# Attention probabilities: 32x32 turns on VectorE and 16 small DMAs in place of transposes on TensorE

## The chip, the cores and the metric

The kernel runs on one core of a Trainium2 chip. Its engines are TensorE (PE, whose weight loads are listed apart as PEld), VectorE (DVE), ScalarE (ACT), GpSimd (POOL) and SyncE (SP), which here only issues DMAs. The metric is the device time of one execution in microseconds. Three runs of the kernel before gave 952.71, 953.46 and 953.47 us, median 953.46.

## The reference

Eight batches of eight heads with 576 positions and head width 64 go through windowed attention: heads 0 to 3 look at the last 32 positions, heads 4 to 7 at every fourth of the last 128. The result goes token by token through an MLP with a rational activation.

```python
scores = scale * np.matmul(q, k.transpose(0, 1, 3, 2))
mask_plain = (rel >= 0) & (rel < window)
mask_dil = (rel >= 0) & (rel < window * dilation) & (rel % dilation == 0)
scores = np.where(masks[None, :, :, :], scores, -1000000000.0)
scores = scores - np.max(scores, axis=-1, keepdims=True)
attn = np.exp(scores)
attn = attn / (np.sum(attn, axis=-1, keepdims=True) + 1e-09)
return np.matmul(attn, v).astype(np.float32)
...
x = np.ascontiguousarray(attn_out.transpose(0, 2, 1, 3)).reshape(B * S, H * D)
...
h = x @ w_in
P = a[0] + a[1] * h + a[2] * h2 + a[3] * h3
Q = 1.0 + np.abs(b[0]) * np.abs(h) + np.abs(b[1]) * h2
g = P / (Q + 1e-06)
return (g @ w_out).astype(np.float32)
```

x has 4608 tokens of width 512; w_in is 512x2048 and w_out 2048x512.

## The kernel before

**Precision.** Every matmul operand of the MLP is split into a high and a low part (`xh`, `xl`, `gh`, `gl`, and two halves of each weight), and each product takes three matmuls: high times high, high times low, low times high.

**The MLP.** The tokens are cut into nine chunks `c` of 512 columns: chunk b (0 to 7) holds the first 512 tokens of batch b, chunk 8 the last 64 tokens of all batches (`x_left`). A chunk takes 16 tiles `ft` of 128 of the 2048 inner columns, 144 tiles in all (class `Tile`). A tile has 12 matmuls into an `h` bank (`Tile.h`), eleven steps of the activation on ACT, DVE and POOL, and 12 matmuls into four `out` banks, issued as four operations of three (`Tile.out`). Both halves are called "halves of a tile" below. Chunk 0 is done in two parts with its partial sums put aside in DRAM (`part`).

**Attention.** A batch is six units (class `Unit`), 48 units in all. Because of the window, and after the dilated heads' positions are put in order modulo 4, each group of 32 queries needs 64 keys. A unit's scores fill 128 partitions by six blocks of 64 keys. The unit's steps are: scores (PE); mask, maximum and subtraction (DVE); exponential (ACT); sum and reciprocal (DVE); `norm` (POOL); `transposes` (PE, three of 128x128 against an identity, into a PSUM bank); `place` (ACT or DVE, from the bank to the SBUF tile `pT`); `av`, attention times values (PE); and the evacuation of the result into `xh` (ACT) and `xl` (DVE).

**Two forms of a unit.** Batches below `ROWS` use matmuls of 128 rows by 64 columns (24 for the scores and 24 for `av`, counting both passes of a float32 matmul). The probabilities are placed in two copies of 64 partitions each into a tile that holds zeros in the other places. For some of these units (`ON_PE`) PE adds the mask by a matmul with the identity, and ACT takes the exponential bank by bank with the maximum as bias and the sum accumulated (`max_bank`, `exp_bank`), so that DVE has no mask, subtraction and sum to do. Batches from `ROWS` on (the attribute `rows`) use matmuls of 64 rows by 32 columns (48 for the scores, 96 for `av`) into two joined PSUM banks (`pair`); one copy places all of `pT`. These units start when all weights have been decoded, since the joined banks take the room of others. In the kernel before `ROWS` is 2.

**Order.** No engine chooses its order at run time. Class `Plan` simulates all operations ahead: each has the engines that may run it with a cost in ns, the operations that it needs, a rank (the time at which it is due, in tiles), and the buffers that it takes (`plan.takes`). The plan always starts what can start first, and of what can start within `WINDOW` ns the lowest rank. Each engine's instructions are then issued in the planned order and wait on semaphores for what they need. `DUE` gives for each batch when its last unit is due and the step between units; `LATE`, `SLACK`, `EARLY_TILES` and `PERIOD` shift ranks. A DMA is booked as its time on SP, then its bytes at 405 bytes per ns, then 1600 ns until it has landed. From the second unit of a form on, `av` of one unit and the scores of the next are one operation `sc` on PE; it needs `prev.placed`.

**SP.** One queue issues all DMAs: loads of q and k (`qk`), of v, of the weights, and stores of outputs from the tiles of the tag `stage` (four buffers, shared with the decoding of the weights). q/k and v have one buffer each, so a unit's loads are issued when the scores or `av` of the unit before have read theirs.

The lines that matter here: 300 to 308 (`scores_rows`), 392 to 403 (`av`), 363 to 389 (`exp` to `place`), 471 to 521 (the unit's operations), 541 to 548 (buffers), 823 and 824 (`pT`).

Of the kernel before, what the change touches and what calls it, by code (L numbers as in the profile page):

```python
# [18 lines left out]
P = 128  # L19
# [6 lines left out]
BOTH, ON_ACT, ON_DVE = {"ACT": 450, "DVE": 500}, {"ACT": 450}, {"DVE": 500}  # L26


ON_PE = [[1, 0, 0, 1, 1, 1], [1, 0, 1, 1, 1, 0], [0, 0, 0, 0, 0, 0], [0, 0, 0, 0, 0, 0], [0, 0, 0, 0, 0, 0], [0, 0, 0, 0, 0, 0], [0, 0, 0, 0, 0, 0], [0, 0, 0, 0, 0, 0]]
PLACE = [(ON_ACT, ON_DVE), (ON_ACT, ON_ACT), (ON_ACT, ON_DVE), (ON_DVE, ON_ACT), (ON_DVE, ON_ACT), (ON_DVE, ON_ACT), (ON_DVE, ON_ACT), (ON_DVE, ON_ACT)]  # L30
DUE = [(1.14, 0.78), (7.17, 0.52), (31.12, 3.35), (44.26, 2.11), (55.98, 1.84), (78.88, 1.84), (93.23, 1.71), (104.69, 0.27)]

LATE = {"ab": -19.97, "ql": -10.42, "pl": 5.4, "qq": 18.68, "t1": 4.2, "t2": -2.51, "ln": -22.56, "ex": -3.7, "g0": 1.26, "g1": 0.06, "g2": -6.38, "gh": -35.31, "gl": 12.35, "out": 3.53}
SLACK = {"sc": -0.4, "qk0": 0.66, "v0": 0.33, "load": -2.47, "wi": 2.03, "wo": 0.71, "w": 0.79, "gl": 0.63, "out": 2.59}

EARLY_TILES = 48

ROWS = 2
LEFT = S - 512
NQ, NKEY, NV = 2 * 6 * 64, 2 * 224, 3 * 2 * 2 * 64  # L40
RQ, RKEY = 4 * 3 * 32, 4 * 128
# [36 lines left out]
class Plan:  # L78
# [1 line left out]


    HOP = {"PE": 200.0, "ACT": 135.0, "DVE": 120.0, "POOL": 80.0, "SP": 0.0}
    TO_POOL, DUE_HOP, WINDOW = 70.0, 150.0, 100.0
    DMA_START, DMA_NS, DMA_RATE = 4000.0, 1600.0, 405.0
    PERIOD = 4051.0

    def __init__(self):
        self.ops, self.tags = [], {}
# [87 lines left out]
def tile_attention_moe(  # L176
# [32 lines left out]
    def mm(o, lhs, rhs, start=True, stop=True):  # L209
        pin(nc.tensor.matmul(o, lhs, rhs, start=start, stop=stop))  # L210
# [44 lines left out]
    class Unit:  # L255
# [97 lines left out]
        def sub(self, pool, tag):  # L353
            self.new_p(pool, tag)
            if self.rows:

                p = self.p.rearrange("p (i r) k -> p r i k", r=2)
# [19 lines left out]
        def transposes(self, tag):  # L377
            self.t = self.bank(tag, "t_ps")
            pf = self.p.rearrange("p j k -> p (j k)")
            for i in range(3):  # L380
                pin(nc.tensor.transpose(self.t[:, P * i : P * i + P], pf[:, P * i : P * i + P], ident))  # L381

        def place(self, half, eng):
            src = self.t[:, :384].rearrange("p (g q) -> p g q", q=32)
            if self.rows:
                copy(eng, pT_rows, self.t[:, :384].rearrange("p (i c) -> p i c", i=3))
                return
            dst = self.pT.rearrange("p i h e q -> p (i h e) q")
            lo = 64 * half
            copy(eng, dst[lo : lo + 64, :, 32 * half : 32 * half + 32], src[lo : lo + 64])  # L390

        def av(self, tag):
            v_t = self.v.rearrange("p (i h e d) -> p i h e d", i=3, h=2, e=2)
            if self.rows:
                for i in range(3):
                    for h in range(2):

                        for n in range(4):
                            for r in range(2):
# [69 lines left out]
        def plan(self, by, start):  # L469

            b, u = self.b, self.u
            alt = u % 2 if start else 0
            self.pT = pTs[alt]
            s_tag, t_tag, self.o_tag = start["banks"] if start else ("att", "att", "dec")
            (qp, qt), (kp, kt), (vpool, self.vt), (pp, pt) = start["tiles"] if start else ((att, "qk"), (att, "qk"), (att, "v"), (att, "p"))
            rows = self.rows
# [48 lines left out]
            if not start:  # L525
                sc.follows.append(Unit.last_read[0])
            Unit.last_read = [Unit.last_read[1], tr]
# [17 lines left out]
            plan.takes(tr, t_tag, PS_BUFS[t_tag], self.placed)  # L545
# [278 lines left out]
    pT_rows = pTs[0].rearrange("p i h e q -> p (i h e q)")[:, :384].rearrange("p (i c) -> p i c", i=3)  # L824
# [163 lines left out]
```

## Time and profile before

| | us |
|---|---|
| median of 3 runs | 953.46 |
| lowest, highest | 952.71, 953.47 |
| the profiled execution | 949.98 |
| its span, from the first to the last instruction | 948.2 |

In the page's rows an engine's name is followed by its busy time; a group's row gives the line, engine and operation, the tile written and the tiles read, the shape, the count, then busy time and mean ns of one, then the engine's idle time ahead of it and what ended it. Many instructions stand under the line of a helper (210 for matmuls, 213 for activations, 216 and 219 for additions and products on DVE, 222 for POOL, 207 for DMAs), so groups are told apart by their tiles: `p` are a unit's probabilities, `p_T` is the tile `pT`, `pair` the joined banks, `h` and `out` the banks of the MLP, `a`, `r`, `t` its intermediate tiles.

A matmul's row in a timeline runs until its modelled end; matmuls overlap, so what one costs is read from the start of the next. A DMA's row on SP is the issue alone; the data lands later.

### The profile page before, as it was taken

The numbers are of one execution on the slowest core, as the hardware profiler recorded it, in microseconds if no ns is written. First come the engines' busy times: TensorE is split into PE (matmuls) and PEld (weight loads), VectorE is DVE, ScalarE is ACT, GpSimd is POOL, SyncE is SP. The second block draws the span as 40 slices with busy tenths as digits, with TensorE's granted clock in tenths as the row PEclk, the third lists the DMA queues.
The fourth block names the chain that finished last, engine by engine and source line by source line (L and its number), as shares of the span: only waits on it lengthen the run. The fifth ranks groups of instructions, "written<-read, shape, count | busy, mean of one in ns | idle before, by whom it ended". The sixth has DMA issues, their size and how long they took to land.

```text
span 948.2 us, 22991 instructions
## 1 busy us (share of the span) xinstructions
PE 905.2 (95%) x9373; PEld 735.1 (78%) x9373; DVE 720.0 (76%) x1301; ACT 677.3 (71%) x1172; POOL 469.3 (49%) x409
## 2 busy tenths in 40 slices
PE   6699788999999999999999999999999999999998
PEld 5577566777778788878888887888888888888876
DVE  5989989667788777887577886778887577666655
ACT  4888788657666666767776767667677787777765
POOL 3666757554545454544544453444344445445442
PEclk9999999999999999999999999999999999999999
DMA  9745800013332212311022122122320010001001
GB/s 337 274 162 182 337 22 1 20 37 119 119 118 74 75 37 84 101 49 33 1 82 66 48 74 75 53 65 75 118 74 19 1 45 1 1 1 45 1 1 45
DMA packets 26025, 72.74 MB, mean 77 GB/s; under 512 B 3008, under 2 KB 3904, under 8 KB 25920
## 3 DMA queue, kind: packets, MB, share of 16 engines
q1 hardware_dynamic: 25920, 71.28, 21.7%
q8 instruction: 73, 1.20, 0.5%
q14 instruction: 32, 0.26, 0.1%
HBM read 60.79 MB, written 10.49 MB: 75 GB/s over the span
## 4 chain that ended last, share of the span: by engine, by line
PE 80%; DVE 10%; ACT 5%; issue 2%; DMA 1%; POOL 1%; SPq 0%; ACTq 0%; POOLq 0%; DVEq 0%
PE h L210 36%; PE out L210 36%; PE pair L210 6%; DVE a L219 2%; ACT r L213 1%; DVE h L219 1%; PE pair L381 1%; DVE xl L216 1%; PE s_ps L210 1%; ACT p L213 1%; DVE mx L337 1%; DVE t L216 1%; ACT t L213 1%; DVE wo_b L219 1%; ACT a L213 1%
## 5 line engine op out<-in xcount | busy, mean ns | idle before, releaser
L210 PE MATMUL h<-xh,wi 128*128 128x512 f32 x1136 | 379.7, 395 | 14.1 <-DVE a L219 12.4
L210 PE MATMUL out<-gh,wo 128*128 128x512 f32 x1136 | 357.8, 396 | 2.3 <-POOL wo L222 1.7
L222 POOL TENSOR_TENSOR a<-r,a 128x512 f32<-128x512 f32 x141 | 182.3, 1293 | 269.8 <-ACT r L213 261.3
L210 PEld LDWEIGHTS h<-xh,wi 128*128 128x128 f32 x1136 | 214.4, 189 | 64.0 <-DVE a L219 18.8
L210 PEld LDWEIGHTS out<-gh,wo 128*128 128x128 f32 x1136 | 208.9, 188 | 48.4 <-POOL wo L222 2.3
L210 PE MATMUL h<-xl,wi 128*128 128x512 f32 x568 | 222.7, 392 | 0.0
L210 PE MATMUL out<-gl,wo 128*128 128x512 f32 x568 | 221.8, 391 | 0.0
L222 POOL TENSOR_TENSOR gl<-a,gh 128x512 fp32r<-128x512 f32 x141 | 185.4, 1315 | 39.2 <-ACT gh L213 38.1
L219 DVE SCALAR_TENSOR_TENSOR a<-a,r 128x512 f32<-128x512 f32 x141 | 98.2, 697 | 114.6 <-ACT r L213 112.4
L213 ACT ACTIVATE r<-a,ln_bias 128x512 f32<-128x512 f32 x141 | 102.2, 725 | 72.5 <-POOL a L222 72.3
L213 ACT ACTIVATE a<-h 128x512 f32<-128x512 f32 x140 | 83.6, 597 | 87.1 <-PE h L210 86.4
L219 DVE SCALAR_TENSOR_TENSOR h<-h,na_t,r 128x512 f32<-128x512 f32 x142 | 107.0, 754 | 43.1 <-ACT r L213 43.0
L210 PEld LDWEIGHTS h<-xl,wi 128*128 128x128 f32 x568 | 107.4, 189 | 23.3 <-issue 2.1
L210 PEld LDWEIGHTS out<-gl,wo 128*128 128x128 f32 x568 | 106.7, 188 | 22.8
L213 ACT ACTIVATE r<-a,ab_t 128x512 f32<-128x512 f32 x141 | 114.7, 813 | 5.5 <-DVE a L219 3.5
L219 DVE SCALAR_TENSOR_TENSOR h<-t,na_t,h 128x512 f32<-128x512 f32 x142 | 107.2, 755 | 4.1
L213 ACT ACTIVATE t<-h,na_t 128x512 f32<-128x512 f32 x142 | 110.0, 774 | 0.1
L213 ACT ACTIVATE r<-r,exp_bias 128x512 f32<-128x512 f32 x144 | 103.8, 721 | 3.6
L216 DVE TENSOR_TENSOR t<-t,h 128x512 f32<-128x512 f32 x142 | 96.9, 682 | 11.2 <-ACT t L213 10.1
L213 ACT ACTIVATE gh<-a 128x512 fp32r<-128x512 f32 x123 | 77.7, 632 | 38.6 <-PE out L210 28.5
L219 DVE SCALAR_TENSOR_TENSOR a<-a,h 128x512 f32<-128x512 f32 x140 | 95.4, 682 | 2.5
L222 POOL TENSOR_TENSOR p<-p,sm 128x384 f32<-128x384 f32 x48 | 40.4, 841 | 79.3 <-DVE sm L372 42.9
(103 smaller groups left out, 726.0 us busy)
## 6 DMA issues: line engine op xcount, KB each, us to landing
v<-in_vp_dram SPq DMA_DIRECT2D x48, 384.0 KB, 3.7
qk<-in_qk_rows_dram SPq DMA_DIRECT2D x36, 448.0 KB, 4.6
out_dram<-os SPq DMA_DIRECT2D x36, 256.0 KB, 2.2
wi_raw<-in_w_in_dram SPq DMA_DIRECT2D x16, 512.0 KB, 8.1
wo_raw<-in_w_out_dram SPq DMA_DIRECT2D x16, 512.0 KB, 8.7
qk<-in_qk_dram SPq DMA_DIRECT2D x6, 608.0 KB, 5.0
q<-in_qk_dram SPq DMA_DIRECT2D x6, 384.0 KB, 6.8
k<-in_qk_dram SPq DMA_DIRECT2D x6, 224.0 KB, 7.0
```

The source lines that it names most:

```text
L210: pin(nc.tensor.matmul(o, lhs, rhs, start=start, stop=stop))
L213: pin(nc.scalar.activation(o, i, func, **kw))
L216: pin(nc.vector.tensor_tensor(o, x, y, op))
L219: pin(nc.vector.scalar_tensor_tensor(o, x, s, y, op0, op1))
L222: pin(nc.gpsimd.tensor_tensor(o, x, y, op))
L337: pin(nc.vector.tensor_reduce(mx, self.blocks(), axis=AX, op=ALU.max))
L381: pin(nc.tensor.transpose(self.t[:, P * i : P * i + P], pf[:, P * i : P * i + P], ident))
```

## The change

From batch 3 on, the units no longer use PE's transposes and the copy out of the bank. `turn` runs two DVE transposes, each on 128x192 elements: within each group of 32 partitions every 32x32 block of the probabilities is turned, and the result goes to a tile `turned` of the tag `stage`. `move` then issues 16 DMAs on SP from SBUF to SBUF, each of 32 partitions by 96 elements (12 KB), which bring block (g, n) from partitions 32g and columns 96n to partitions 32n and columns 96g of `pT`. Units with an odd number put `pT` into one of the two buffers of tag `p`, the others into the old tile. `av` reads its operand at other columns; its matmuls have the same number and shape. The subtraction writes `p` in the order (r, i) instead of (i, r).

Batch 2 goes back to the form of batches 0 and 1, with the mask on PE for five of its six units. In batch 1 the mask is on PE for six units instead of four; in batch 0 for four as before, but others. The constants of the plan (`PLACE`, `DUE`, `LATE`, `SLACK`, `EARLY_TILES`, `WINDOW`, `PERIOD`, and the cost of `sc`) are changed too. In the plan, the moves are booked at 2400 ns on SP and three times their bytes.

```diff
-ON_PE = [[1, 0, 0, 1, 1, 1], [1, 0, 1, 1, 1, 0], [0, 0, 0, 0, 0, 0], [0, 0, 0, 0, 0, 0], [0, 0, 0, 0, 0, 0], [0, 0, 0, 0, 0, 0], [0, 0, 0, 0, 0, 0], [0, 0, 0, 0, 0, 0]]
+ON_PE = [[0, 0, 1, 1, 1, 1], [1, 1, 1, 1, 1, 1], [1, 0, 1, 1, 1, 1], [0, 0, 0, 0, 0, 0], [0, 0, 0, 0, 0, 0], [0, 0, 0, 0, 0, 0], [0, 0, 0, 0, 0, 0], [0, 0, 0, 0, 0, 0]]
...
-DUE = [(1.14, 0.78), (7.17, 0.52), (31.12, 3.35), (44.26, 2.11), (55.98, 1.84), (78.88, 1.84), (93.23, 1.71), (104.69, 0.27)]
+DUE = [(0.94, 0.39), (7.47, 0.67), (31.59, 4.01), (46.12, 2.31), (58.3, 2.05), (80.22, 2.04), (96.72, 1.88), (106.06, 0.47)]
...
-EARLY_TILES = 48
-
-ROWS = 2
+EARLY_TILES = 36
+
+ROWS = 3
...
+        def turn(self):
+
+            self.turned = work.tile([P, 512], F32, tag="stage", name=f"u{self.n}", bufs=4)[:, :384]
+            src = self.p.rearrange("p (r i) (k a) -> p r k i a", r=2, k=2)
+            dst = self.turned.rearrange("p (r k i q) -> p r k i q", r=2, k=2, i=3)
+            for r in range(2):
+                pin(nc.vector.transpose(dst[:, r], src[:, r]))
+
+        def move(self):
+
+            if self.n % 2:
+                self.pT = att.tile([P, 6, 64], F32, tag="p", name=f"pT{self.n}", bufs=2).rearrange("p j k -> p (j k)")
+            else:
+                self.pT = pTs[0].rearrange("p i h e q -> p (i h e q)")[:, :384]
+            for n in range(4):
+                for g in range(4):
+                    load(self.pT[32 * n : 32 * n + 32, 96 * g : 96 * g + 96], self.turned[32 * g : 32 * g + 32, 96 * n : 96 * n + 96])
...
-                                c0, c1 = 192 + 96 * h + 32 * i, 64 * h + 32 * e
-                                mm(pair[0][32 * n : 32 * n + 32, r, c0 : c0 + 32], v_t[half, i, h, e, d], pT_rows[half, i, c1 : c1 + 32])
+                                c0, c1 = 192 + 96 * h + 32 * i, 96 * (2 * h + e) + 32 * i
+                                mm(pair[0][32 * n : 32 * n + 32, r, c0 : c0 + 32], v_t[half, i, h, e, d], self.pT[half, c1 : c1 + 32])
...
-                sc = op({"PE": 1370 if rows else 1750 + cost}, 0, lambda e: (prev.av(prev.o_tag), scores()), *prev.placed, prev.lv, *ready)
+                sc = op({"PE": 1650 if rows else 1750 + cost}, 0, lambda e: (prev.av(prev.o_tag), scores()), *prev.placed, prev.lv, *ready)
...
-            tr = op({"PE": 350 * cold}, 0, lambda e: self.transposes(t_tag), no, identity)
-            p0 = op(place0, 0, lambda e: self.place(0, e), tr, zeroed[alt], Unit.av_of.get(alt))
-            self.placed = [p0]
-            if not rows:
+            if rows:
+                tr = op({"DVE": 540}, 0, lambda e: self.turn(), no)
+                mv = op({"SP": 2400}, 0, lambda e: self.move(), tr, dma=P * 384 * 4 * 3)
+                self.placed = [mv]
+            else:
+                tr = op({"PE": 350 * cold}, 0, lambda e: self.transposes(t_tag), no, identity)
+                p0 = op(place0, 0, lambda e: self.place(0, e), tr, zeroed[alt], Unit.av_of.get(alt))
                 p1 = op(place1, 0, lambda e: self.place(1, e), tr, zeroed[alt], Unit.av_of.get(alt))
-                self.placed.append(p1)
+                self.placed = [p0, p1]
...
+            if rows:
+                plan.takes(tr, "stage", 4, [mv])
+            else:
+                plan.takes(tr, t_tag, PS_BUFS[t_tag], self.placed)
...
+            if self.rows:
+                plan.takes(self.placed[0], *(("p", 2) if self.n % 2 else ("pT", 1)), [av])
```

More of the change, by code (lines that the diff above doesn't have):

```diff
@@ L26 @@
 BOTH, ON_ACT, ON_DVE = {"ACT": 450, "DVE": 500}, {"ACT": 450}, {"DVE": 500}
-ON_PE = [[1, 0, 0, 1, 1, 1], [1, 0, 1, 1, 1, 0], [0, 0, 0, 0, 0, 0], [0, 0, 0, 0, 0, 0], [0, 0, 0, 0, 0, 0], [0, 0, 0, 0, 0, 0], [0, 0, 0, 0, 0, 0], [0, 0, 0, 0, 0, 0]]
-PLACE = [(ON_ACT, ON_DVE), (ON_ACT, ON_ACT), (ON_ACT, ON_DVE), (ON_DVE, ON_ACT), (ON_DVE, ON_ACT), (ON_DVE, ON_ACT), (ON_DVE, ON_ACT), (ON_DVE, ON_ACT)]
-DUE = [(1.14, 0.78), (7.17, 0.52), (31.12, 3.35), (44.26, 2.11), (55.98, 1.84), (78.88, 1.84), (93.23, 1.71), (104.69, 0.27)]
-LATE = {"ab": -19.97, "ql": -10.42, "pl": 5.4, "qq": 18.68, "t1": 4.2, "t2": -2.51, "ln": -22.56, "ex": -3.7, "g0": 1.26, "g1": 0.06, "g2": -6.38, "gh": -35.31, "gl": 12.35, "out": 3.53}
-SLACK = {"sc": -0.4, "qk0": 0.66, "v0": 0.33, "load": -2.47, "wi": 2.03, "wo": 0.71, "w": 0.79, "gl": 0.63, "out": 2.59}
-EARLY_TILES = 48
-ROWS = 2
+ON_PE = [[0, 0, 1, 1, 1, 1], [1, 1, 1, 1, 1, 1], [1, 0, 1, 1, 1, 1], [0, 0, 0, 0, 0, 0], [0, 0, 0, 0, 0, 0], [0, 0, 0, 0, 0, 0], [0, 0, 0, 0, 0, 0], [0, 0, 0, 0, 0, 0]]
+PLACE = [(BOTH, BOTH), (ON_ACT, ON_ACT), (ON_DVE, ON_ACT), (ON_ACT, ON_DVE), (ON_ACT, ON_DVE), (ON_ACT, ON_DVE), (ON_ACT, ON_DVE), (ON_ACT, ON_DVE)]
+DUE = [(0.94, 0.39), (7.47, 0.67), (31.59, 4.01), (46.12, 2.31), (58.3, 2.05), (80.22, 2.04), (96.72, 1.88), (106.06, 0.47)]
+LATE = {"ab": -8.55, "ql": -4.01, "pl": -1.52, "qq": -2.86, "t1": 1.53, "t2": -0.78, "ln": -21.92, "ex": -13.06, "g0": 2.39, "g1": 0.11, "g2": -10.17, "gh": -21.84, "gl": 13.45, "out": 3.38}
+SLACK = {"sc": -0.39, "qk0": -0.2, "v0": -0.54, "load": -2.56, "wi": 1.44, "wo": 0.87, "w": 0.4, "gl": 0.78, "out": 2.83}
+EARLY_TILES = 36
+ROWS = 3
 LEFT = S - 512
@@ L82 @@
     HOP = {"PE": 200.0, "ACT": 135.0, "DVE": 120.0, "POOL": 80.0, "SP": 0.0}
-    TO_POOL, DUE_HOP, WINDOW = 70.0, 150.0, 100.0
+    TO_POOL, DUE_HOP, WINDOW = 70.0, 150.0, 200.0
     DMA_START, DMA_NS, DMA_RATE = 4000.0, 1600.0, 405.0
-    PERIOD = 4051.0
+    PERIOD = 4743.0
     def __init__(self):
@@ L355, in sub @@
             if self.rows:
-                p = self.p.rearrange("p (i r) k -> p r i k", r=2)
+                p = self.p.rearrange("p (r i) k -> p r i k", r=2)
                 mx = self.mx.rearrange("p (r i) -> p r i", r=2)
@@ L381, in transposes @@
                 pin(nc.tensor.transpose(self.t[:, P * i : P * i + P], pf[:, P * i : P * i + P], ident))
+        def turn(self):
[12 more added lines that the diff above has]
+                    load(self.pT[32 * n : 32 * n + 32, 96 * g : 96 * g + 96], self.turned[32 * g : 32 * g + 32, 96 * n : 96 * n + 96])
         def place(self, half, eng):
             src = self.t[:, :384].rearrange("p (g q) -> p g q", q=32)
-            if self.rows:
-                copy(eng, pT_rows, self.t[:, :384].rearrange("p (i c) -> p i c", i=3))
-                return
             dst = self.pT.rearrange("p i h e q -> p (i h e) q")
@@ L472, in plan @@
             alt = u % 2 if start else 0
-            self.pT = pTs[alt]
+            if not self.rows:
+                self.pT = pTs[alt]
             s_tag, t_tag, self.o_tag = start["banks"] if start else ("att", "att", "dec")
@@ L526, in plan @@
                 sc.follows.append(Unit.last_read[0])
-            Unit.last_read = [Unit.last_read[1], tr]
+            Unit.last_read = [Unit.last_read[1], su if rows else tr]
             loads = (lq, lk, lv) if start else (lq, lv)
@@ L544, in plan @@
             plan.takes(sc, s_tag, PS_BUFS[s_tag], [su, *(clear[1:] if rows else [])])
-            plan.takes(tr, t_tag, PS_BUFS[t_tag], self.placed)
+            if rows:
+                plan.takes(tr, "stage", 4, [mv])
+            else:
+                plan.takes(tr, t_tag, PS_BUFS[t_tag], self.placed)
             plan.takes(su, pt, 2 if pp is att else 1, [tr])
```

1 line of the change is left out of this document (removed).

## The prediction

> **What bounds the kernel now.** I read the page first (busy shares, the 40 slices), then the busy time by stretches, then the chain that ended last.
>
> ```profile
> span 948.2 us, 22991 instructions
> PE 905.2 (95%) x9373; PEld 735.1 (78%) x9373; DVE 720.0 (76%) x1301; ACT 677.3 (71%) x1172; POOL 469.3 (49%) x409
> PE 80%; DVE 10%; ACT 5%; issue 2%; DMA 1%; POOL 1%; SPq 0%; ACTq 0%; POOLq 0%; DVEq 0%
> ```
> ```profile
> 100.00:175.00 75.00, 65.54 (x315) 50.51 (x315) 69.39 (x114) 58.99 (x97) 49.38 (x40) 0.98 0.24 92
> 175.00:300.00 125.00, 121.95 (x1737) 97.94 (x1740) 93.76 (x176) 82.20 (x136) 61.06 (x56) 1.00 0.25 81
> 300.00:700.00 400.00, 396.41 (x5109) 323.69 (x5098) 310.37 (x585) 278.44 (x457) 187.81 (x161) 1.00 0.20 66
> 700.00:930.00 230.00, 229.51 (x1381) 189.20 (x1380) 154.33 (x243) 172.55 (x265) 109.00 (x85) 1.00 0.05 16
> ```
> The columns of the second fence are the stretch, its length, then the busy time of PE, PEld, DVE, ACT and POOL, the clock and the DMA share. From 175 us to 930 PE is busy 747.9 of 755 us: TensorE is the bound there, and every microsecond of its work that goes is worth about one. From 100 to 175 DVE is (69.4 of 75), while PE idles 9.5. DVE has 22% free from 300 on, and the DMA engines 80%.
>
> What one attention unit costs PE is read from the chain in one dense stretch (start, length, what; x12 is half a tile of the MLP):
>
> ```profile
> 495.88 2.74 PE h L210 x12
> 498.62 2.73 PE out L210 x12
> 501.36 0.33 PE pair L381 x3
> 501.68 2.75 PE h L210 x12
> 504.44 1.45 PE pair L210 x91
> 505.89 2.94 PE out L210 x12
> 508.83 2.72 PE h L210 x12
> ```
> From 495.88 to 508.83 stand four halves (2.72 each undisturbed) and one unit: 12.95 - 10.88 = 2.07 us. The three transposes are 0.33 plus 0.03 by which the next half is longer: 0.36. The remaining 1.7 is attention times values with the next unit's scores (1.45, and 0.22 on the half behind it).
>
> **The change, part by part.**
>
> *Transposes off PE.* Batches 3 to 7 are 30 units: 30 x 0.36 = **-10.8 us**, all of it on the bound.
>
> *Turn on DVE.* The copy out of the bank goes, two transposes of 128x192 come.
>
> ```profile
> L225 DVE COPY p_T<-pair 128x384 f32<-128x384 f32 x30 | 16.6, 554 | 4.6 <-PE pair L381 4.6
> L216 DVE TENSOR_TENSOR pair<-pair,mask_t 128x192 f32<-128x192 f32 x36 | 13.2, 366 | 1.1
> ```
> Each is bounded by half the copy (0.28) and by the 128x192 addition (0.37); I take 0.28, since one input is read as in the copy, so 0.55 against 0.55. DVE's load stays, covered by the 22% that it has free; without that cover the dearer end would cost 30 x 0.18 = 5 us.
>
> *The 16 moves, and PE's new wait.* The matmuls of attention times values now wait for DMAs, not for DVE. Behind them in PE's queue stand the next scores and the MLP's matmuls, for which ACT and DVE wait in turn. The plan fixes the order ahead and books the moves at 2400 + 1456 + 1600 = 5456 ns (SP, bytes, landing). If they take longer, PE stands still by the excess, less the slack that the place in the order happens to leave. No row shows a DMA of 32 rows from SBUF to SBUF; the nearest are:
>
> ```profile
> L207 SPq DMA_DIRECT2D v<-in_vp_dram x48: 327/328/431, 4.5 to 718.3; - x48
> 34.73 0.33 SPq L207 DMA_DIRECT2D qk<-in_qk_dram  x1
> 35.10 1.10 SPq L207 DMA_DIRECT2D wo_raw<-in_w_out_dram  x1
> mask_t<-in_mask_dram SPq DMA_DIRECT2D x1, 96.0 KB, 2.0
> coef_t<-in_coef_dram SPq DMA_DIRECT2D x1, 3.0 KB, 1.7
> ```
> Issuing a DMA of 128 rows keeps SP 0.33 us, the next can start 0.37 after it, and up to 0.43 is seen behind another; the smallest lands 1.7 us after its issue. So from one move to the next it is 0.08 us (a quarter of 0.33 for a quarter of the rows) at the least and 0.48 (0.43 with the same pause) at the most; the 16th lands after 15 of these and 1.7: 2.9 to 8.9 us. I take 0.27, halfway, nearer to the alone-standing 0.33: part of that time should go with the rows. That is 5.75, with 0.2 for SP's pick-up 0.5 late against the booking. The slack is read from when the copy ended and when the matmuls began:
>
> ```profile
> 501.72 0.56 DVE L225 COPY p_T<-pair 128x384 f32<-128x384 f32 x1 [0.22 <-PE pair L381]
> 504.37 0.99 PE L210 MATMUL pair<-p_T,v 64*32 64x32 f32 x94
> 410.86 0.55 DVE L225 COPY p_T<-pair 128x384 f32<-128x384 f32 x1
> 411.71 0.99 PE L210 MATMUL pair<-p_T,v 64*32 64x32 f32 x94
> ```
> 2.09 and 0.30 us: it depends on whether a half of 2.72 us happened to run. I take it as evenly spread from 0 to 2.4. A lateness L then stalls PE by L x L / 4.8 on average: 0.05 us a unit for 0.5, **+2 us** in all, 0 to +72 at the ends (3.6 late is 2.4 a unit over the spread's mean of 1.2).
>
> The Trainium skill's page "DMA: Bandwidth & Descriptors", in the table under "Why a DMA increments its semaphore by 16 and not by 1", gives a copy's issue as 512 sequencer cycles whatever its size, in generations before the newest; with the 1.2 GHz of "Trainium Kernel Development and Optimization", Hardware Hierarchy, that is an estimate of 0.43 us an issue. The trace has 0.43 only behind another DMA and 0.33 alone; a fixed cost is the rule that speaks against this change, and the second rival below is its case.
>
> *Semaphores.* Where one writer was waited for, now up to 16 are.
>
> ```profile
> L381 PEldq EVENT_SEMAPHORE  x3: 51/51/51, 26.1 to 91.1; - x3
> ```
> A wait of its own costs PE's queue 51 ns: 0 to 16 x 0.051 = 0.82 us a unit. The first sixteen matmuls need all sixteen moves, many waits can be met while the array still has work, so I take two of them, 0.1 a unit: **+3 us**, 0 to +24.5 at the ends.
>
> *Moves in SP's queue.* They wait for the turn, and what stands behind them waits too: loads of the next unit and stores of outputs. Loads are issued behind the scores:
>
> ```profile
> 505.43 0.33 SPq L207 DMA_DIRECT2D v<-in_vp_dram  x1
> 505.92 1.47 SPq L207 DMA_DIRECT2D qk<-in_qk_rows_dram  x1
> 518.35 0.33 SPq L207 DMA_DIRECT2D v<-in_vp_dram  x1
> ```
> SP has nothing from 507.39 to 518.35, which is where the moves fall, so I cost this at 0. The cover is gone where an output store is placed ahead of the moves and its copy is late; then it is part of the lateness.
>
> A unit also becomes longer: from the transposes' start to its matmuls it took 504.37 - 501.36 = 3.0 us, and turn, pick-up and moves are 0.55 + 5.95 = 6.5. 30 x 3.5 = 105 us must fit between and behind the units:
>
> ```profile
> 425.62 1.22 SPq L207 DMA_DIRECT2D qk<-in_qk_rows_dram  x1
> 493.82 0.34 SPq L207 DMA_DIRECT2D v<-in_vp_dram  x1
> L225 DVE COPY x_left<-pair x30: 195/214/283, 226.7 to 733.8; 128x32 f32<-128x32 f32 x24, 128x128 f32<-128x128 f32 x6
> ```
> Between these two loads 68 us pass where the dense rhythm has 13: 55 us lie idle in the row of units. The last unit is out at 734, and the last 32 tiles need 32 x 5.44 = 174 us before the end at 948: 40 us more. 95 of the 105 are there in these two places alone, and smaller gaps stand between other batches, so I cost this at 0; without them 10 us of MLP would come late.
>
> *Batch 2 as in batch 1.* A unit there costs PE:
>
> ```profile
> 56.46 0.92 PE L210 MATMUL o_ps<-p_T,v 128*64 128x64 f32 x24
> 57.31 0.34 PE L210 MATMUL s_ps<-mask_t,ident_b 128*128 128x384 bf16 x1
> 57.58 0.92 PE L210 MATMUL s_ps<-qk 128*64 128x64 f32 x24
> 58.43 0.50 PE L210 MATMUL h<-xh,wi 128*128 128x512 f32 x1
> ```
> 0.85 + 0.27 + 0.85, with 0.36 of transposes 2.33, against 2.07 now. Five of six units add the mask on PE: 5 x 0.26 = **+1.3 us**; 0 to +3 with the pauses around it.
>
> *The start.* Batch 1 puts two more units' masks on PE, which takes from DVE the mask, the subtraction and the sum:
>
> ```profile
> L216 DVE TENSOR_TENSOR pair<-pair,mask_t 128x384 f32<-128x384 f32 x18 | 10.2, 564 | 0.6 <-ACT xh L213 0.2
> L216 DVE TENSOR_TENSOR p<-pair,mx 128x384 f32<-128x384 f32 x36 | 20.0, 555 | 0.8
> L368 DVE TENSOR_REDUCE sm<-p 128x6 f32<-128x384 f32 x40 | 22.0, 550 | 1.4 <-ACT p L213 1.2
> ```
> 2 x 1.67 = 3.3 us less on DVE where DVE is the bound; ACT takes them up. All ranks of the plan change as well, which can help or hurt the 9.5 us of PE's idle time there. I take **-1**, -4 to +4.
>
> The sum: -10.8 + 2 + 3 + 1.3 - 1 = -5.5 us. The profiled execution took 949.98 (948.2 of span and 1.8 around it), so 944.5 by its own measure; the median of the runs shown is 953.46, 3.5 above, and I put the same difference on it: **948.0 us**, 0.6% faster.
>
> **Rivals.**
>
> *The whole gain:* moves land within the booking, waits are met early, the start gives its 4 us. -10.8 + 1.3 - 4 = -13.5 at best, about 942 with half of it. For it: a quarter of the rows. Against: sixteen issues in 2.4 us is 0.15 each, under half of any issue in the trace.
>
> *Issue cost that does not shrink (slower):* each move keeps SP for 0.37 us as the 128-row DMAs do. The 16th lands after 15 x 0.37 + 1.7 + 0.2 = 7.5 us, 2.0 late; PE stands before attention times values 2.0 x 2.0 / 4.8 = 0.83 us a unit, +25 us: -10.8 + 25 + 3 + 1.3 - 1 = +17.5, about 971. It decides from the point where stalls eat 5.5 + 2 us, 0.25 a unit, 1.1 late, 0.31 us from one move to the next. For it: loads of different size (v, and qk at 34.73) take SP the same 0.33 us in the trace. Against: all of those have 128 rows.
>
> *Semaphores on PE:* all sixteen waits exposed, +24.5 for +3: 969. Against: the order lets PE's queue run ahead.
>
> *The start turns against it:* +4 for -1 and 1 to 2 more in batch 2: 953 to 956.
>
> **Chances.** Forecast 0.40 (its own range 943 to 953), whole gain 0.14, fixed issue cost 0.28, semaphores 0.06, start 0.12. About 0.2% (1.9 us) is what a measurement of this kernel can tell from no change. Faster: 0.33 of the forecast and 0.14; same: 0.07 of the forecast and 0.07 of the start; slower: 0.28 + 0.06 + 0.05. The range takes in the whole gain and the middle of the fixed issue cost: 941 to 974.
>
> **What would show it.** The transposes of line 381 fall from 48 units to 18, PE's busy time in 300 to 700 is filled by more tiles. Right is the forecast if the gap from the turn's end to the first matmul of attention times values is about 6 us and PE's waits for a DMA there sum to a few us. The slower rival shows as 16 issues on SP at 0.37 us and PE waiting for the last of them, 0.5 to 1 us in most of the 30 units. A lead of eight or more event waits on PE ahead of each unit would show the third. PE idle before 175 us beyond the 9.5 us of 100 to 175 shows the start wrong.

## The result, and the profile after

| | before | after |
|---|---|---|
| median (us) | 953.09 | 1132.61 |
| lowest, highest | 951.17, 953.47 | 1130.36, 1133.15 |
| the profiled execution: span | 948.2 | 1130.9 |
| mean granted clock of TensorE | 0.993 | 0.915 |

Four runs each. The ratio is 1.188 (95% interval 1.186 to 1.191): 18.8% slower. The forecast was 948.0 us and the range ended at 974.

The page of the kernel after, its busy shares, granted clock and chain:

```profile
span 1130.9 us, 22729 instructions
PE 981.9 (87%) x8717; PEld 789.0 (70%) x8717; DVE 733.7 (65%) x1320; ACT 691.5 (61%) x1244; POOL 473.1 (42%) x408
PEclk9899999998899988889998878988988899999999
PE 43%; SPq 17%; DVE 12%; ACT 9%; DMA 8%; issue 6%; POOL 4%; ACTq 0%; POOLq 0%; DVEq 0%
p_T<-u SPq DMA_DIRECT2D x240, 12.0 KB, 1.7
pT<-u SPq DMA_DIRECT2D x240, 12.0 KB, 1.8
```

SP's queue and DMAs, 1% of the chain before, are 25% of it now. The moves land 1.7 to 1.8 us after their issue, which is what the forecast took. PE has 656 instructions fewer, since the transposes and most of batch 2's small matmuls went, and yet it is busy for 77 us more: in the clock row stand many an 8 and a 7, and matmuls at a lower clock take longer.

The busy time by stretches of the kernel after (columns as before: stretch, length, PE, PEld, DVE, ACT, POOL, clock, DMA share, GB/s):

```profile
0.00:100.00 100.00, 78.01 (x770) 62.17 (x770) 81.13 (x167) 72.91 (x214) 57.82 (x66) 0.93 0.59 209
100.00:175.00 75.00, 68.88 (x325) 54.36 (x326) 67.90 (x102) 61.23 (x112) 46.41 (x38) 0.95 0.37 147
300.00:700.00 400.00, 335.50 (x3616) 268.39 (x3615) 234.24 (x446) 210.76 (x342) 137.50 (x114) 0.88 0.18 53
700.00:930.00 230.00, 188.76 (x2132) 151.23 (x2132) 130.94 (x251) 114.94 (x189) 74.40 (x61) 0.87 0.18 54
```

From 100 to 175 nothing is lost (PE 68.9 busy where it was 65.5). From 300 to 700 PE idles 64.5 us where it idled 3.6, at a clock of 0.88 where it was 1.00. The loss lies behind the start, where the units of batches 3 to 7 run.

One unit in the timeline (start, length, engine and line, what, and in brackets the idle time ahead and what ended it):

```profile
617.76 0.63 DVE L388 STREAM_TRANSPOSE u<-p 128x192 f32<-128x192 f32 x2
618.16 10.01 SPq L207 DMA_DIRECT2D p_T<-u  x16
624.88 0.24 PE L210 MATMUL pair<-p_T,v 64*32 64x32 f32 x2
627.51 0.34 PE L210 MATMUL pair<-p_T,v 64*32 64x32 f32 x8 [2.39 <-DMA p_T<-u]
628.23 0.41 PE L210 MATMUL pair<-p_T,v 64*32 64x32 f32 x8 [0.38 <-DMA p_T<-u]
628.83 0.41 PE L210 MATMUL pair<-p_T,v 64*32 64x32 f32 x8 [0.19 <-DMA p_T<-u]
630.03 0.92 PE L210 MATMUL pair<-p_T,v 64*32 64x32 f32 x69 [0.79 <-DMA p_T<-u]
631.63 1.22 PE L210 MATMUL out<-gh,wo 128*128 128x512 f32 x2
633.07 0.63 PE L210 MATMUL h<-xh,wi 128*128 128x512 f32 x1
633.50 0.63 PE L210 MATMUL h<-xl,wi 128*128 128x512 f32 x1
635.59 0.39 PE L210 MATMUL h<-xl,wi 128*128 128x512 f32 x1
635.82 0.63 PE L210 MATMUL h<-xh,wi 128*128 128x512 f32 x2
```

The reader is to see three things. First, SP is at the sixteen moves for 10.0 us, 0.63 each; the plan had booked 2.4 us there and 5.5 until all are landed. Second, PE arrives at 624.88 by the planned order, starts two matmuls whose move has landed, and stands still for 3.75 of the next five microseconds, released move by move; until 631.63 the unit keeps PE 6.75 us, where before it took 1.45 (504.44 to 505.89 in the prediction's chain). Third, after that stop the MLP's matmuls start 0.43 us apart (633.07, 633.50), and from about 635 on 0.23 again (635.59, 635.82): the clock had been lowered. The same unit by stretches (columns as above) shows the clock at 0.50 from 628.18 to 635.00:

```profile
624.80:628.18 3.38, 0.66 (x11) 0.36 (x10) 2.14 (x4) 1.77 (x3) 1.07 (x1) 1.00 0.08 18
628.18:635.00 6.82, 5.79 (x142) 4.77 (x143) 2.06 (x4) 1.34 (x3) 1.28 (x1) 0.50 0.39 124
635.00:640.00 5.00, 5.00 (x23) 4.12 (x23) 2.87 (x8) 2.97 (x6) 1.30 (x1) 1.00 0.04 14
```

The waits grouped (who, at what line, for what: us in total, times, longest):

```profile
PE pair L210 <- DMA pT<-u: 54.8, 56, 3.5
PE pair L210 <- DMA p_T<-u: 48.5, 56, 3.6
PE pair L210 <- issue: 10.7, 7, 1.8
```

PE's waits for moves are 103.3 us in all; the forecast said "a few". Another 10.7 stand at the same units with no releaser named. Half of the moves on SP (min/median/max of one issue in ns, first and last start; the other half has the same median), beside the loads of v with 128 rows from DRAM:

```profile
L207 SPq DMA_DIRECT2D p_T<-u x240: 507/588/1434, 253.0 to 897.1; - x120
L207 SPq DMA_DIRECT2D v<-in_vp_dram x48: 327/333/1502, 13.0 to 900.0; - x48
```

A move of a quarter of the rows takes longer to issue than a full load: 0.588 us against 0.333.

### The profile page after: what moved, and what is told of

Its sections match the earlier page's. It is cut to its first block, busy times and chain, and to the rows that moved or that the text cites. A ratio compares the mean times of both kernels' runs of the same rounds, so it can differ in the third digit from the quotient of the medians.

```text
span 1130.9 us, 22729 instructions
## 1 busy us (share of the span) xinstructions
PE 981.9 (87%) x8717; PEld 789.0 (70%) x8717; DVE 733.7 (65%) x1320; ACT 691.5 (61%) x1244; POOL 473.1 (42%) x408
## 4 chain that ended last, share of the span: by engine, by line
PE 43%; SPq 17%; DVE 12%; ACT 9%; DMA 8%; issue 6%; POOL 4%; ACTq 0%; POOLq 0%; DVEq 0%
PE out L210 19%; PE h L210 18%; SPq L207 17%; ACT r L213 5%; PE pair L210 5%; DVE a L219 3%; DVE h L219 3%; DMA p_T<-u 3%; POOL a L222 2%; DMA pT<-u 2%; DMA v<-in_vp_dram 1%; ACT a L213 1%; DVE t L216 1%; POOL p L222 1%; DMA wi_raw<-in_w_in_dram 1%
## 5 line engine op out<-in xcount | busy, mean ns | idle before, releaser
L210 PE MATMUL h<-xh,wi 128*128 128x512 f32 x1136 | 391.1, 406 | 9.2 <-DVE a L219 8.8
L210 PE MATMUL out<-gh,wo 128*128 128x512 f32 x1136 | 374.1, 412 | 0.0
L210 PEld LDWEIGHTS h<-xh,wi 128*128 128x128 f32 x1136 | 223.9, 197 | 63.2 <-DVE a L219 12.2
L210 PEld LDWEIGHTS out<-gh,wo 128*128 128x128 f32 x1136 | 221.9, 199 | 50.8 <-issue 5.2
L210 PE MATMUL out<-gl,wo 128*128 128x512 f32 x568 | 230.2, 405 | 1.3 <-POOL gl L222 1.3
L210 PE MATMUL h<-xl,wi 128*128 128x512 f32 x568 | 229.1, 403 | 0.8 <-DVE xl L216 0.8
L219 DVE SCALAR_TENSOR_TENSOR a<-a,r 128x512 f32<-128x512 f32 x141 | 103.3, 732 | 115.2 <-ACT r L213 106.9
L210 PEld LDWEIGHTS out<-gl,wo 128*128 128x128 f32 x568 | 112.4, 198 | 26.7 <-POOL gl L222 1.9
L210 PEld LDWEIGHTS h<-xl,wi 128*128 128x128 f32 x568 | 112.1, 197 | 24.3 <-DVE xl L216 1.1
L216 DVE TENSOR_TENSOR pair<-pair,mask_t 128x192 f32<-128x192 f32 (+1 forms) x45 | 19.5, 433 | 117.0 <-ACT xh L213 116.0
```

What stands on the lines that cost most here:

```text
L216: pin(nc.vector.tensor_tensor(o, x, y, op))
L219: pin(nc.vector.scalar_tensor_tensor(o, x, s, y, op0, op1))
```

## The experiments

The theory: a move's issue costs 0.63 us because both its ends are in SBUF, sixteen need 10 us, and PE stops by what that exceeds the booking and the slack of the order. The rivals: the many small packets; a limit on transfers under way; the plan's new constants; the turn.

**The issue by itself.** A small kernel with nothing but DMAs on SP, in groups: sixteen SBUF to SBUF (eight of 32 rows, eight of 128), four of 128 x 96, eight of 64 rows; then sixteen from DRAM (32 and 128 rows), eight to DRAM, four from DRAM with four pieces a row, four SBUF to SBUF of 32 x 2 KB.

> No attention and no MLP: SP alone issues groups of DMAs of nine forms, 4 to 8 of each, one behind the other: SBUF to SBUF with 32, 64 and 128 partitions, DRAM to SBUF with 32 and 128, SBUF to DRAM with 32, and 32 partitions with four runs each or with 2 KB rows. In the changed kernel a 32-partition SBUF-to-SBUF issue took 0.588 us, in the kernel before a 128-partition load or store 0.33. Theory 1 (both ends in SBUF make it dear): SBUF to SBUF takes about 0.59 us with 32, 64 and 128 partitions alike, and 32 partitions to or from DRAM about 0.33. Theory 2 (few rows, or a start partition other than 0, make it dear): 32 partitions take about 0.59 us wherever the ends are, and 128 partitions from SBUF to SBUF 0.33. Theory 3 (the queue is full in the big kernel): here all forms take 0.33 to 0.43 us.

Its timeline on SP (start, time from the first to the end of the last, what, count):

```profile
1.42 10.16 SPq L27 DMA_DIRECT2D sb<-src  x16
11.62 2.53 SPq L27 DMA_DIRECT2D sb128w<-src  x4
14.20 5.07 SPq L27 DMA_DIRECT2D sb<-src  x8
19.31 7.75 SPq L27 DMA_DIRECT2D ld<-in_w_dram  x16
27.11 3.68 SPq L27 DMA_DIRECT2D far<-src  x8
30.82 1.84 SPq L27 DMA_DIRECT2D ld32x<-in_w_dram  x4
32.71 2.45 SPq L27 DMA_DIRECT2D sb32w<-src  x4
```

And the durations of one issue by form, as above:

```profile
L27 SPq DMA_DIRECT2D sb<-src x24: 569/594/600, 1.4 to 18.7; - x24
L27 SPq DMA_DIRECT2D ld<-in_w_dram x16: 419/426/718, 19.3 to 26.6; - x16
```

From SBUF to SBUF one takes 0.62 to 0.64 with its pause, on average of each group, whether it has 32, 64 or 128 rows and 192 bytes or 2 KB a row. With one end in DRAM it takes 0.46 to 0.48 (all but the first load), again whatever its rows and pieces. So rows, bytes and packets are ruled out; the pair of ends sets the price. The first theory's 0.33 for the forms with one end in DRAM was too low: behind another one an issue takes 0.42 to 0.43.

**PE's transposes put back into the kernel after.** All else, the constants, batch 2 and the masks on PE, is as after:

```diff
...
-                tr = op({"DVE": 540}, 0, lambda e: self.turn(), no)
-                mv = op({"SP": 2400}, 0, lambda e: self.move(), tr, dma=P * 384 * 4 * 3)
-                self.placed = [mv]
+                tr = op({"PE": 350}, 0, lambda e: self.transposes(t_tag), no, identity)
+                self.placed = [op(ON_DVE, 0, lambda e: self.place(0, e), tr, zeroed[alt], Unit.av_of.get(alt))]
...
```

> The changed kernel with the transposes on PE and the single copy (on DVE) put back from batch 3 on; batch 2's form, the masks on PE and all constants of the plan stay as changed. Theory (the moves are the cause, the rest of the change is worth little): within 1% of the kernel before, 945 to 962 us, so 170 to 188 us faster than the changed kernel. Rival (the new constants and batch 2's form cost a good part): 985 us or more.

954.74 us, ratio 1.002 (1.001 to 1.003) to before. The constants, batch 2 and the start together, with an order of their own, are worth about 2 us of loss (0.7 to 3.2); turn and moves hold the rest of the 180.

**All the moves, but nobody waits for them.** The sixteen moves are issued as after, into places that are not read; attention times values reads a tile that holds zeros.

```diff
-                self.pT = pTs[0].rearrange("p i h e q -> p (i h e q)")[:, :384]
+                self.pT = pTs[0].rearrange("p i h e q -> p (i h e q)")[:, 384:]
...
-                                mm(..., self.pT[half, c1 : c1 + 32])
+                                mm(..., pTs[0].rearrange("p i h e q -> p (i h e q)")[half, c1 : c1 + 32])
```

> The changed kernel in the same planned order with all turns and all 480 moves, but the moves go to places that nobody reads, and attention times values reads a tile of zeros that is long there: the attention's result is left out, only PE's wait for the moves is gone. Theory (PE standing still for the moves, and the slower clock behind each stop, are all of the loss): 935 to 955 us, granted clock back at 0.98 or more. Rival 1 (the moves disturb others: SP's queue late for loads and stores, DMA traffic, DVE's waits on the stage buffers): 980 us or more although PE no longer waits. Rival 2 (sixteen semaphore waits on PE's own queue cost most): also gone here, so it is told apart by the profile of the changed kernel, not by this run.

953.72 us, ratio 1.002 (1.001 to 1.004). PE's wait for the moves is thus nearly all of the loss. (With the moves, PE's wait for the turn and the steps ahead of it is gone too; the run with four moves below has these waits and shows that they cost nothing.) Yet the time is no better than before, although the transposes are gone. Where the rest went, its timeline shows:

```profile
575.68 12.03 SPq L207 DMA_DIRECT2D pT<-u  x16
587.82 2.55 SPq L207 DMA_DIRECT2D out_dram<-os  x4
589.32 0.69 DVE L225 COPY os<-out 128x512 f32<-128x512 f32 x1 [6.62 <-DMA pT<-u]
590.07 1.22 PE L210 MATMUL out<-gh,wo 128*128 128x512 f32 x2 [5.59 <-DVE os L225]
```

The turned tile holds one of the four stage buffers for 12 us. A chunk's outputs come at that time; the copy of one of them finds no buffer until the last move has been read, and PE waits 5.6 us for the copy.

**The moves booked at what they take**, 10.45 us with landing:

```diff
-                mv = op({"SP": 2400}, 0, lambda e: self.move(), tr, dma=P * 384 * 4 * 3)
+                mv = op({"SP": 8000}, 0, lambda e: self.move(), tr, dma=P * 384 * 7)
```

> The changed kernel with the moves booked in the plan at 8.0 us of SP and 10.4 us until they have landed, instead of 2.4 and 5.5, so that the plan puts attention times values later. Nothing else is changed. Theory A (the booking is the fault; PE has other work to put ahead): PE's waits for the moves fall to under 1.5 us a unit and the time to 945 to 985 us. Theory B (thirty units of some 22 us do not fit ahead of the tiles that need them): PE's waits move to the ends of the batches, and the time stays above 1040 us.

1128.84 us, ratio 1.187 (1.180 to 1.193) to before: hardly better. Its stretches, and its largest waits:

```profile
0.00:100.00 100.00, 54.97 (x689) 44.61 (x689) 48.37 (x122) 53.08 (x194) 24.19 (x35) 0.78 0.54 190
100.00:175.00 75.00, 21.75 (x80) 17.20 (x81) 65.41 (x95) 30.19 (x47) 55.94 (x56) 0.63 0.40 159
300.00:700.00 400.00, 355.57 (x3995) 283.82 (x3997) 259.06 (x493) 244.55 (x412) 161.09 (x135) 0.94 0.22 65
```
```profile
PE h L210 <- DVE a L219: 73.9, 12, 52.8
PE pair L210 <- DMA pT<-u: 33.3, 20, 7.1
PE pair L210 <- DMA p_T<-u: 1.5, 5, 0.4
```

From 300 to 700 PE is 20 us busier than after, but in the first 175 us it loses 70 (76.7 busy, 146.9 after): the start has another order, and in one place PE stands 52.8 us for DVE's `a` of a tile. That the longer chain changed that order is likely, but not shown. A true booking moves the loss; with these constants it does not remove it. Of both theories a part came true: PE's waits for the moves fall from 103.3 to 34.8 us, the four longest stops stand six units, a batch, apart, and the time stays high.

In 16 of the 29 units between 245 and 925 us PE does not stop at all, though each has its sixteen moves, at the same 10 us on SP. One of them:

```profile
386.76 1.27 PE L210 MATMUL pair<-p_T,v 64*32 64x32 f32 x94
388.49 0.50 PE L210 MATMUL h<-xh,wi 128*128 128x512 f32 x1
```

It keeps PE 1.73 us. So it is the lateness behind the order that stops PE, not the number of moves or of waits for them.

**No moves at all.** The turn stays, attention times values reads zeros:

```diff
-            for n in range(4):
-                for g in range(4):
-                    load(self.pT[32 * n : 32 * n + 32, 96 * g : 96 * g + 96], self.turned[32 * g : 32 * g + 32, 96 * n : 96 * n + 96])
+            self.pT = pTs[0].rearrange("p i h e q -> p (i h e q)")[:, :384]
```

> The changed kernel without any move: turns on DVE as before, attention times values reads a tile of zeros, so that the attention's result is left out. The planned order is the same as with the moves. The run without waits kept the moves and gave 953.7 although the transposes are gone from PE; there stores of outputs stood behind the moves in SP's queue and waited for their buffers. Theory A (the 10.8 us of transposes are a real gain, and the moves' 10 us a unit on SP and in the stage buffers ate it): 941 to 947 us. Theory B (the transposes were worth less than their row says, or the turns on DVE cost as much): 950 to 955 us.

934.83 us, ratio 0.982 (0.980 to 0.984), lower than either theory said. This is the floor of the idea: what the change would give if the blocks came to their places for nothing. (PE does not wait for the turn here; that the floor holds with this wait, four moves will show.) It lies 16.5 us below the median of the kernel before that was taken with it, 951.30. Two of its stretches:

```profile
100.00:175.00 75.00, 71.27 (x344) 56.84 (x345) 69.20 (x106) 63.78 (x113) 51.52 (x41) 0.98 0.35 139
300.00:700.00 400.00, 398.60 (x5161) 323.49 (x5160) 322.67 (x617) 293.65 (x477) 191.37 (x157) 1.00 0.21 66
```

PE is full from 300 to 700, with two DVE transposes in every unit: the turn costs PE nothing.

**Four, eight and twelve moves** in place of sixteen. Four move all 128 partitions by 96 elements, eight 64 partitions by 96; twelve are eight of 32 partitions and four of 64. The bytes are the same in all.

```diff
-            for n in range(4):
-                for g in range(4):
-                    load(self.pT[32 * n : 32 * n + 32, 96 * g : 96 * g + 96], self.turned[32 * g : 32 * g + 32, 96 * n : 96 * n + 96])
+            for g in range(4):
+                load(self.pT[:, 96 * g : 96 * g + 96], self.turned[:, 96 * g : 96 * g + 96])
```

> The changed kernel with 4 moves of 128 partitions by 96 elements instead of 16 of 32: the same bytes and packets, every place of the tile written, but blocks stay in their 32 partitions, so the attention's result is wrong and left out. Plan and waits as changed. By the run of issue forms 4 x 0.64 + 1.8 + 0.15 = 4.5 us against the 5.5 booked. Theory (the number of issues decides, not bytes or packets): no waits, 943 to 955 us. Rival (the small packets of 384 bytes or DMA traffic decide): over 1000 us.

> The same with 8 moves of 64 partitions by 96 elements; blocks again land in other places than the result needs. By the run of issue forms 8 x 0.64 + 1.8 + 0.15 = 7.1 us against 5.5 booked: 1.6 late. Theory (lateness beyond the booking less the slack of 0 to 2.4 us): 0.5 us of standing still a unit, with the slower clock behind it 15 to 25 us above the four-move run, 958 to 980 us. Rival (loss in proportion to the number of moves, half of the changed kernel's): about 1040 us.

> The changed kernel with twelve moves in place of sixteen: eight of 32 partitions for the first half of the columns, four of 64 partitions for the second, each with the same 96 columns. All of the tile is still written, but the second half's blocks stay in their places, so the result of attention is left out. Asked is the shape of the loss between eight moves (947.5 us) and sixteen (1132.6). At 0.633 us a move the last lands at 0.2 + 11 x 0.633 + 1.7 = 8.9 us after the turn, 3.4 behind the plan's booking of 5.46; with eight it was 0.9, with sixteen 5.9. Theory A, the loss goes straight with the lateness between the two: (8.9 - 6.3) / (11.4 - 6.3) x 185 + 947.5 = about 1040 us, PE stopped 2.5 to 3 us a unit. Theory B, lateness less a slack of 1.2 on average (this is how I had reckoned it): 2.2 us a unit, 66 in all and 10 to 15 of slower clock: about 1010 to 1025. Rival, sixteen is a step of its own (something that holds about sixteen transfers is full): twelve behave as eight do, 950 to 965.

| moves | the last lands after the booking (us) | PE per unit (us) | median (us) |
|---|---|---|---|
| 0 | | 1.45 | 934.83 (932.82 to 936.04) |
| 4 | -1.8 | 1.45 | 935.61 (934.98 to 938.42) |
| 8 | 0.9 | 1.84 | 947.48 (943.46 to 951.97) |
| 12 | 3.4 | 4.01 | 1027.24 (1025.76 to 1029.25) |
| 16 | 5.9 | 6.77 | 1132.61 (1130.36 to 1133.15) |

The second column is worked out: 0.2 for SP's pick-up, 0.633 from one move to the next (0.60 for four), 1.7 to land, less the 5.456 booked. By the traces, from the end of the turn to the landing of the last move, it is -1.9, 0.7, 3.5 and 5.7 on average: the first moves start 0.23 us before the turn's end, since they need its first half alone. The third is the mean from the first matmul of attention times values to the first of the MLP behind it, over the units between 245 and 925 us. In the waits for the moves, the larger of two rows with eight moves (7.2 us in both):

```profile
PE pair L210 <- DMA p_T<-u: 5.2, 12, 1.0
```

and with twelve (50.6 in both):

```profile
PE pair L210 <- DMA pT<-u: 26.8, 55, 2.1
```

No step lies at sixteen: the loss begins where the last move lands after the booking, is small while the slack of the order covers it, and then grows by about as much as the lateness. From eight to twelve moves the lateness grows by 2.5 us and the unit by 2.2, from twelve to sixteen by 2.5 and 2.8. For twelve the straight line of theory A (1040) is off by 13, lateness less the mean slack (1010 to 1025) by 2, though the unit grew by 2.6 us where that theory had 2.2. For eight the forecast of 958 to 980 was too high: they cost 12 us more than four, not 15 to 25. Four came out below their forecast of 943 to 955.

**The turned tile in a place of its own**, in the kernel whose moves nobody waits for. Its moves go to the unit's own `p`, so that no other buffer is held either; the two edits aren't told apart.

```diff
-            self.turned = work.tile([P, 512], F32, tag="stage", name=f"u{self.n}", bufs=4)[:, :384]
+            self.turned = pTs[0].rearrange("p i h e q -> p (i h e q)")[:, 384:]
...
+            self.pT = self.p.rearrange("p j k -> p (j k)")
...
```

> The kernel in which all sixteen moves are issued and nobody waits for them (953.7 us), with the turned blocks kept in a place of their own in place of one of the four stage buffers, which the output stores and the left-over tiles use too, and with the moves going to the unit's own probabilities, which are no longer needed. Attention times values reads zeros, so its result is left out. Theory A, the 10 to 19 us that lie between this and the kernel without moves (934.8) come through the stage buffers, which a turned tile holds for 10 us longer than planned: 935 to 941 us, and PE's waits for DVE's and ACT's copies to the stage tiles, 9.2 us in all, fall to 1 to 3. Theory B, SP's queue itself does it, stores and loads stand behind 10 us of moves whatever buffer they use: 948 to 954, and those waits stay at 5 to 10.

937.24 us, ratio 0.985 (0.983 to 0.987), 16.5 us less than with the stage buffer. The waits for the copies to the stage tiles:

```profile
ACT os L213 <- PE out L210: 2.3, 2, 2.0
DVE os L225 <- PE out L210: 0.9, 1, 0.9
```

PE's waits for these copies are gone, and the copies wait for PE alone. SP's queue issues the same 480 moves, 2.4 us behind the kernel without any, so the queue by itself costs little; held buffers were the way of the side effect.

**By way of DRAM.** The turned tile is stored whole to DRAM and loaded by four DMAs, each filling 32 partitions in four pieces; five issues in place of sixteen, none from SBUF to SBUF.

```diff
-            for n in range(4):
-                for g in range(4):
-                    load(self.pT[32 * n : 32 * n + 32, 96 * g : 96 * g + 96], self.turned[32 * g : 32 * g + 32, 96 * n : 96 * n + 96])
+            far = dram.tile([P, 384], F32, name=f"far{self.n}")
+            load(far, self.turned)
+            for n in range(4):
+                load(self.pT[32 * n : 32 * n + 32].rearrange("p (g c) -> p g c", g=4), far[:, 96 * n : 96 * n + 96].rearrange("(g p) c -> p g c", g=4))
...
-                mv = op({"SP": 2400}, 0, lambda e: self.move(), tr, dma=P * 384 * 4 * 3)
+                mv = op({"SP": 4400}, 0, lambda e: self.move(), tr, dma=P * 384)
```

> The changed kernel, its result the same, but the 16 moves become five DMAs by way of a scratch array in DRAM: one store of the turned tile (128 rows), then four loads of 32 partitions with four runs of 384 bytes each; the plan books 4.4 us of SP and 6.1 us until they have landed. From the run of issue forms an issue to or from DRAM takes SP 0.42 us and lands 1.9 us after it: 0.42 + 2.0 of waiting for the store + 4 x 0.47 + 1.9 = 6.2 us instead of 12. Theory (the price of the moves is their SBUF-to-SBUF issue, 16 times 0.63 us): PE's waits for the moves nearly vanish and the time is 943 to 956 us. Rival (a DMA between turn and matmul is too late whatever its price): 1000 us or more.

947.59 us, ratio 0.9967 (0.9947 to 0.9987), as the theory said. Its units keep PE 1.76 us on average, where they take 1.45 without moves: six of the thirty still stop, for 0.6 to 2.3 us. That is some 10 of the 13 us by which it lies above the floor. With the turned tile kept apart from the stage buffers as above:

> The version by way of DRAM (one store, four loads, 947.6 us) with the turned blocks in a place of their own in place of a stage buffer. The whole computation is done. Theory A, stage buffers matter: 3 to 7 us less, 940 to 945 us. Theory B, they do not, since here a buffer is held for 2 us only: 946 to 949.

947.54 us, ratio 0.9953 (0.9939 to 0.9967): no difference, as the rival said. Both compute all of the result and are 0.3 to 0.5% faster than before. One unit of the first on SP:

```profile
500.94 0.33 SPq L207 DMA_DIRECT2D far<-u  x1
502.86 1.75 SPq L207 DMA_DIRECT2D pT<-far  x4
```

From the store's issue to the end of the last load's it takes 3.7 us, with the store's landing in between; the sixteen moves need 10.0 for their issues.

## Why the prediction was wrong

**The step that failed** is *The 16 moves, and PE's new wait*: "from one move to the next it is 0.08 us ... at the least and 0.48 ... at the most", taken as 0.27. It is 0.633, above the upper bound. The bounds came from loads out of DRAM, and the reason for the value taken, that "part of that time should go with the rows", is refuted: 32 and 128 rows cost the same. The rival *issue cost that does not shrink* had the right mechanism with 0.37 us, again the price of a load.

With 0.633 in the prediction's own sums (its 0.2 for SP's pick-up included, though the first moves start before the turn's end) the sixteenth lands 15 x 0.633 + 1.7 + 0.2 = 11.4 us after the turn, 5.94 behind the booking; less the mean slack of 1.2 that is 4.7 us a unit, 142 in all, and 953.5 - 10.8 + 142 + 3 + 1.3 - 1 = 1088 us. So this one price makes 140 of the 185 us by which the forecast was low. The terms without the moves, -10.8 + 1.3 - 1, give 943.0 where the floor is 934.8, so 8 us of the loss were hidden by an error the other way. The rest:

- *Slack taken as evenly 0 to 2.4*: a unit keeps PE 6.77 - 1.45 = 5.3 us longer, 160 in all, 18 more than that sum. Of these 114 are idle time of PE (103.3 and 10.7); the rest is matmuls of the unit itself, started in pieces and in part at the lower clock.
- *The clock behind each stop*, which no step had. In the MLP's matmuls between 245 and 925 us the time by which starts lie further apart than 0.227 adds up to 44 us, against 10 in the kernel without moves: +34. Hardly any of the 44 is idle time: most starts of this kind are 0.43 apart, and 27, the first two matmuls behind a unit, 0.59. The trace: a stop of some 5 us with a few short matmuls in it, then 0.43 in place of 0.23 until 635.00, 5 us after the restart at 630. The Trainium skill's page "TensorE: Matmul & The Clock Gate", section "What's actually happening", says that the array goes to half its clock after an idle window of about 3.4 us, and back after such a window of work. By the granted clock of 0.50 for 6.8 us, twice 3.4, the trace agrees; but in the 3.4 us ahead of 628.18 ten short matmuls ran and no idle time was over 2.39 us, so here a window that was not empty was enough.
- *Moves in SP's queue*, costed at 0 with the words "The cover is gone where an output store is placed ahead of the moves". The other way round it was: the turned tile kept the outputs out of their buffers. Without PE's wait this is 953.7 - 937.2 = 16.5 us. In the kernel after, none of it shows: one copy by ACT waits 6.0 us for a move, but the MLP's matmuls into `out` stand idle for no copy.

160 + 34 = 194 of the 198 us between 934.8 and 1132.6.

**What held.** *Transposes off PE*, -10.8: the direction is right. The floor is 18.3 us below the median before, 16.5 below the one taken with it, so 6 to 8 us more than the forecast; no run takes the transposes off alone. PE is busy 3.3 us longer than before from 100 to 175 in the kernel after and 5.7 in this one, so *the start*, taken as -1, may hold some 4 of them. That the same constants with PE's transposes give 954.7 and not 945.6 (934.8 + 10.8) stays open; that version has another order of operations.

*Turn on DVE*, 0: right that it costs PE nothing, but a piece takes 355 ns, near the dear end of its bounds (0.28 to 0.37) and not the cheap one that was taken:

```profile
L388 DVE STREAM_TRANSPOSE u<-p 128x192 f32<-128x192 f32 x60 | 19.0, 355 | 5.3 <-POOL p L222 5.2
```

*Semaphores*, +3: four waits that are met early cost nothing that shows (935.6 against 934.8). Sixteen do, in the run with the moves booked: its units without a stop keep PE 1.72 to 1.76 us instead of 1.45, some 0.28 a unit or 8 in all, inside the bounds of 0 to 24.5. That the waits make all of it is not shown: with moves under way and no wait for them a unit takes 1.65. In the kernel after these 8 are part of the 160. *Landing*, 1.7: right (1.7 to 1.8). *A unit becomes longer* by 3.5 us at no cost: in the unit shown it became longer by 9.3 (from 617.76 to 630.03 against 3.0), and when the plan is told, the order that it makes loses as much at the start. *Batch 2*, +1.3: with the start and the constants +2 where +0.3 was forecast.

The Trainium skill's page "DMA: Bandwidth & Descriptors" had, in the section cited, a fixed price for an issue, an estimate of 0.43 us with the 1.2 GHz that "Trainium Kernel Development and Optimization" gives under NeuronCore Architecture (not under the heading that the prediction names). It holds for a DMA with one end in DRAM behind another (0.42 to 0.43), and that it does not go with the size holds for all forms tried; for SBUF to SBUF the measured 0.59 decides.

## What to carry to other kernels

Count DMA issues, not bytes: price each by a row with the same two ends, and where no such row exists, let the upper bound be open, since a price that sixteen issues multiply decides the sign. Where an order is fixed ahead, a booking that is short costs nothing up to the slack of the place, and behind it about every microsecond of lateness in each unit, with the lowered clock on top. And a buffer shared with other work is held until the last slow DMA has read it: look who asks for it meanwhile.

## What the runs showed of the hardware

In the run of issue forms the issue on SP of a DMA from SBUF to SBUF keeps the queue 0.55 to 0.60 us (0.62 to 0.64 to the next), with one end in DRAM 0.42 to 0.43 behind another; a load alone takes 0.33 in the kernel after. With both ends in SBUF it is the same for 32, 64 and 128 rows and for 192 bytes to 2 KB a row; with one in DRAM the same for 32 and 128 rows. Why the ends matter wasn't tried. By way of DRAM and back is thus the shorter way for sixteen blocks: 3.7 us on SP from the first issue to the last, where the direct way takes 10.0.

Short waits among small matmuls can lower TensorE's clock too. With twelve moves PE was busy 2.26 us with 130 instructions, most of them 64x32 and 64x64 matmuls, between 412.76 and 416.17, and idle for 0.40 at most at a time; from 416.17 to 419.58 the granted clock was 0.50. In the kernel without moves, where the same matmuls run without a wait, it is 1.00 from 300 to 700.
